# One load for K and V of the last kv head, and its softmax factors and outputs apart from those of the first seven heads

## The chip, the cores and the metric

The kernel runs on one core of one Trainium2 chip. The metric is the device time of one execution in microseconds (us). TensorE (PE in the profile; PEld is its weight load), VectorE (DVE), ScalarE (ACT), GpSimd (POOL) and SyncE (SP) run side by side, each through its own instructions in a fixed order, and wait for each other by semaphores. All loads are issued by SP and run on 16 DMA engines. All data is float32.

## The reference

One decode step of attention over a cached window, a dense block with the Mish activation beside it, and a gate that mixes the two. Two batch rows, 32 query heads on 8 kv heads, head size 128, a window of the last 4096 keys.

```python
def _A_ref(x, k_cache, v_cache, wq, wo):        # x (2, 1, 512), Hq 32, Hkv 8, Dh 128
    W = min(4096, max(256, Sk // 4))            # 4096 of 32768 keys
    rep = Hq // Hkv                             # 4
    q = ((x @ wq).reshape(B, Sq, Hq, Dh)).transpose(0, 2, 1, 3)
    k = jnp.repeat(k_cache[:, :, Sk - W:, :], rep, axis=1)
    v = jnp.repeat(v_cache[:, :, Sk - W:, :], rep, axis=1)
    scores = jnp.einsum("bhqd,bhkd->bhqk", q, k) * (Dh ** -0.5)
    p = _softmax(scores, axis=-1)
    o = jnp.einsum("bhqk,bhkd->bhqd", p, v)
    return o.transpose(0, 2, 1, 3).reshape(B, Sq, Hq * Dh) @ wo
def _B_ref(x, w1, b1, w2):                      # F 1792
    h = jnp.einsum("bsd,df->bsf", x, w1) + b1
    sp = jnp.log1p(jnp.exp(-jnp.abs(h))) + jnp.where(h > 0, h, jnp.zeros_like(h))
    return jnp.einsum("bsf,fd->bsd", h * jnp.tanh(sp), w2)
g = _sigmoid((x * gate_w).sum(-1, keepdims=True))
return g * a + (1 - g) * b
```

## The kernel before, in words

**Loads.** The pool `stream` has three buffers of 64 KB per partition. In order of issue they take: wq; K and V of kv heads 0 to 6 (`kv0` to `kv6`, each one load of 128 rows of 64 KB); `w12`, which is w1 and ten of the fourteen slabs of w2 (rows of 48 KB); `kv7`, which is K of the last head (rows of 32 KB) and then V of it (another 32 KB); and `wo` in three loads for kv heads 0 to 3, 4 to 6 and 7 (`WO`, rows of 32, 24 and 8 KB). Three small loads of the last slabs of w2 come last, into the free end of w12's buffer (L282). A load of a buffer waits until the last matmul on what the buffer held is done: `wo` waits for the values of `kv6`. SP issues everything, so the order of the loads is the order of the program.

**One kv head.** `scores` (L137) multiplies the queries with K, 16 matmuls in groups of four: four matmuls stand in four column groups of 32 of the array (`Q * j`) and run side by side. The profile shows each float32 matmul as two records, so a group of four is eight. VectorE takes the row maximum (`mx`), ScalarE the exponential and the row sum (`p`, `ls`). `turned` (L149) transposes p by four matmuls into `pp`, and ScalarE copies it to `pT`. `values` (L162) multiplies pT with V, 16 matmuls in groups of four, into half of a two-head tile of PSUM; after an odd head VectorE picks the valid part of both heads (`om`, L175) and sums it (`od`, L178).

**The softmax across pieces.** A row of a head is spread over several pieces with a maximum of their own. `tops` (L181) transposes the maxima of all eight heads (`mt`), copies them (`ms`), takes the common one (`mj`, `top`), subtracts on GpSimd and takes the exponential; `factors` (L197) transposes that back (`ft`) into `kf` and `kl`; `shares` (L208) sums by a matmul (`lp`) and inverts (`r`); `outputs` (L217) does one small matmul per head (`ol`) and scales into `oT`.

**The end.** `hidden` (L225) does the first layer of the dense block as w12 lands. Then, in an order that is written out by hand and pinned on TensorE (`pin`): scores of head 7, five slabs of w2 (`middle`), `tops`, the transposes of head 7, five slabs of w2, `factors`, the values of head 7 with `shares` in between, `outputs`, and 32 matmuls of oT with wo (`project`, L290; four query heads to a kv head, again four side by side). The sum `acc` is copied (`asum`), added up over its four column groups together with the last four slabs of w2 (`fin`), copied to `res` and stored.

Of the kernel before, what the change touches and what calls it, by code (L numbers as in the profile page):

```python
# [20 lines left out]
DH = 128
W = min(4096, max(256, SK // 4))
NH = 2
# [15 lines left out]
CAP = 20.0  # L39
CUTS = (0, 10, 12, 13, 14)  # L40
WO = (0, 4, 7, 8)


@with_exitstack
def decode_kernel(ctx: ExitStack, tc: tile.TileContext, res, stored, small, wqh, wqt, kv_in, w12, k7, v7, wo, w2, out):
    nc = tc.nc

    stream = ctx.enter_context(tc.tile_pool(name="stream", bufs=3))
# [8 lines left out]
    def load(name, *parts):  # L57
        t = stream.tile([P, 2 * CHUNK], F32, tag="s", name=name)
        x = 0
        for cols, src in parts:  # L60
            loads.append(nc.sync.dma_start(t[:, x : x + cols], src))  # L61
            x += cols
        return t
# [93 lines left out]
    def softmax(kv, t):  # L157
        return turned(kv, scores(kv, t))

    pair = [None]  # L160

    def values(kv, pT, t, c0=0, c1=NT):  # L162
        if kv % 2 == 0:
            pair[0] = ps_1.tile([P, 2, BN * DH], F32, tag="o", name=f"o{kv}")
        o = pair[0][:, kv % 2, :]
        for c in range(c0, c1):
            for j in range(NJ):
                pin(nc.tensor.matmul(o[Q * j : Q * j + Q], pT[:, c, Q * j : Q * j + Q],  # L168
                                     t[:, (c * NJ + j) * 512 : (c * NJ + j + 1) * 512],
                                     start=(c == 0), stop=(c == NT - 1)))  # L170
        if kv % 2 and c1 == NT:
            wide = [P, 2 * BN, DH]
            om = single.tile(wide, F32, tag="om", name=f"om{kv}")
            ov = om.rearrange("p (k m) d -> p k m d", m=BN)
            nc.vector.tensor_tensor(  # L175
                ov, pair[0].rearrange("p k (m d) -> p k m d", m=BN),
                pick[:, None, :, None].to_broadcast([P, 2, BN, DH]), op=ALU.mult)
            nc.vector.tensor_reduce(od[:, kv - 1 : kv + 1], ov.rearrange("p k m d -> p k d m"),  # L178
                                    axis=AX.X, op=ALU.add)

    def tops():  # L181
        mt = ps_1.tile([HKV, NJ, Q], F32, tag="q", name="mt")
        pin(nc.tensor.transpose(mt.rearrange("k j r -> k (j r)"), mx, ident))
        ms = const.tile([HKV, NJ, Q], F32, name="ms")
        nc.scalar.copy(ms, mt)
        m4 = ms.rearrange("k j (y n h) -> k j y n h", n=NH, h=REP)
        mj = const.tile([HKV, NJ, Q // NH // REP, REP], F32, name="mj")
        nc.vector.tensor_tensor(mj, m4[:, :, :, 0, :], m4[:, :, :, 1, :], op=ALU.min)
        top = const.tile([HKV, Q // NH // REP, REP], F32, name="top")
        nc.vector.tensor_reduce(top, mj.rearrange("k j y h -> k y h j"), axis=AX.X, op=ALU.min)  # L190
        for n in range(NH):
            nc.gpsimd.tensor_tensor(m4[:, :, :, n, :], m4[:, :, :, n, :],
                                    top[:, None].to_broadcast(mj.shape), op=ALU.subtract)
        nc.scalar.activation(ms, ms, AF.Exp, scale=-1.0)
        return ms

    def factors(ms):  # L197
        ft = ps_1.tile([P, HKV], F32, tag="q", name="ft")
        pin(nc.tensor.transpose(ft, ms.rearrange("k j r -> k (j r)"), ident[:HKV, :HKV]))
        wide = [P, HKV, BH]  # L200
        kb = key.rearrange("p b h -> p (b h)")[:, None, :].to_broadcast(wide)
        kf = const.tile(wide, F32, name="kf")
        kl = const.tile(wide, F32, name="kl")
        nc.vector.tensor_tensor(kf, kb, ft[:, :, None].to_broadcast(wide), op=ALU.mult)
        nc.vector.tensor_tensor(kl, kf, ls[:, :, None].to_broadcast(wide), op=ALU.mult)
        return kf, kl

    def shares(kl):  # L208
        lp = ps_1.tile([P, HKV, B, REP], F32, tag="q", name="lp")
        pin(nc.tensor.matmul(lp.rearrange("p k b h -> p (k b h)"), ones,  # L210
                             kl.rearrange("p k x -> p (k x)"), start=True, stop=True))
        r = const.tile([P, HKV, B, REP], F32, name="r")
        nc.vector.reciprocal(r, lp)
        nc.gpsimd.tensor_tensor(r, r, g[:, None, :, None].to_broadcast([P, HKV, B, REP]), op=ALU.mult)
        return r

    def outputs(ol, kf, r, k0, k1):  # L217
        for kv in range(k0, k1):
            pin(nc.tensor.matmul(ol[:, kv].rearrange("p b h -> p (b h)"), od[:, kv, :], kf[:, kv, :],  # L219
                                 start=True, stop=True))  # L220
        nc.vector.tensor_tensor(
            oT.rearrange("p (k h) (b x) -> p k b h x", h=REP, x=RS)[:, k0:k1, :, :, 0],
            ol[:, k0:k1], r[:, k0:k1], op=ALU.mult)

    def hidden(t):  # L225
        w = t[:, : DC * F].rearrange("p (c f) -> p c f", c=DC)
        hp = ps_s.tile([P, FG * P], F32, tag="sc", name="hp")
        for c in range(DC):
            for j in range(NJ):
                n = min(FG, FC - j * FG) * P  # L230
                nc.tensor.matmul(hp[Q * j : Q * j + Q, :n], x32[:, c, :],  # L231
                                 w[:, c, j * FG * P : j * FG * P + n],
                                 start=(c == 0), stop=(c == DC - 1))
        hs = work.tile([P, FG * P], F32, tag="p", name="hs")
        nl = (FC - (NJ - 1) * FG) * P
# [24 lines left out]
        nc.gpsimd.tensor_scalar_add(de, nu, 2.0)  # L260
        nc.vector.reciprocal(de, de)
        nc.gpsimd.tensor_tensor(nu, nu, de, op=ALU.mult)
        nc.gpsimd.tensor_tensor(actT[:, :, ::RS], nu, ho, op=ALU.mult)
# [1 line left out]
    queries(0, wq_t[:, :CHUNK])  # L265
    queries(1, wq_t[:, CHUNK:])

    for kv in range(HKV - 1):
        t = load(f"kv{kv}", (2 * CHUNK, kv_in[kv]))
        pT = softmax(kv, t[:, :CHUNK])  # L270
        values(kv, pT, t[:, CHUNK:])
    w12_t = load("w12", (DC * F + CUTS[1] * D, w12))
    last = load("kv7", (CHUNK, k7), (CHUNK, v7))

    def flat(src, cuts, size):
        for f0, f1 in zip(cuts, cuts[1:]):
# [4 lines left out]
    for cols, src in flat(w2, [f - CUTS[1] for f in CUTS[1:]], D):  # L281
        loads.append(nc.sync.dma_start(w12_t[:, x : x + cols], src))  # L282
        x += cols
    hidden(w12_t)

    acc = ps_1.tile([P, D], F32, tag="acc", name="acc")
    fin = ps_1.tile([P, P], F32, tag="fin", name="fin")
# [19 lines left out]
            x = DC * F + f * D  # L307
            pin(project(f % NJ, actT[:, f, :], w12_t[:, x : x + D], n_of[f % NJ]))

    p = scores(HKV - 1, last[:, :CHUNK])  # L310
    middle(0, CUTS[1] // 2)
    ms = tops()
    pT = turned(HKV - 1, p)
    middle(CUTS[1] // 2, CUTS[1])
    kf, kl = factors(ms)
    values(HKV - 1, pT, last[:, CHUNK:], 0, 1)
    r = shares(kl)
    values(HKV - 1, pT, last[:, CHUNK:], 1, NT)
    ol = ps_1.tile([P, HKV, B, REP], F32, tag="q", name="ol")
    outputs(ol, kf, r, 0, HKV - 2)  # L320
    outputs(ol, kf, r, HKV - 2, HKV)
    for x in range(HQ):
        project(x % REP, oT[:, x, :], wo_t[:, x * D : (x + 1) * D], n_of[x % REP])
    asum = work.tile([P, D], F32, tag="p", name="asum")
    nc.scalar.copy(asum[:, : D // 2], acc[:, : D // 2])
    nc.vector.tensor_copy(asum[:, D // 2 :], acc[:, D // 2 :])
# [76 lines left out]
```

## Time and profile before

| what | value |
|---|---|
| median of 3 runs | 219.33 us (219.29 to 219.65) |
| the profiled execution, its own time | 219.44 us |
| its span in the profile | 217.6 us, so 1.84 us lie around it |
| bytes moved | 91.40 MB, mean 420 GB/s over the span |
| busy: PE | 119.1 us (55%) |
| busy: PEld, DVE, ACT, POOL | 34.6, 21.9, 15.4 and 7.5 us |

Times in the rows below are microseconds from the start of the span. A row of the timeline gives start, length, engine, line, operation, what is written and read, the shapes, how many records are merged, and in brackets how long the engine had been idle and what ended that. The length of a merged row runs from its first start to its last end. A matmul's end is modelled, so of matmuls the starts are read first. The granted clock is a share of 2.4 GHz.

### The profile page before, as it was taken

The page shows a single profiled execution, that of the slowest core. Times are in us where ns is not written, and L with a number is a line of the kernel's source. Part 1 is how long each engine was busy: PE and PEld are TensorE (multiplying, and loading weights), DVE is VectorE, ACT ScalarE, POOL GpSimd, SP SyncE. Part 2 cuts the span into 40 slices and gives each one's busy share as a digit, 9 for nine tenths or more (in the row PEclk, how much of TensorE's full clock was granted, in tenths as well). Part 3 has the DMA queues.
Part 4 walks back from the last instruction along what each step waited for, and adds up shares of the span by engine and source line. Part 5 has one row for each costly group of instructions (what it writes and reads, how often), then busy time and mean ns, then how long its engine had stood idle before and what let it go on. Part 6 is the DMA issues. An engine that isn't in the chain of part 4 may idle for free.

```text
span 217.6 us, 1803 instructions
## 1 busy us (share of the span) xinstructions
PE 119.1 (55%) x804; PEld 34.6 (16%) x804; DVE 21.9 (10%) x34; ACT 15.4 (7%) x34; POOL 7.5 (3%) x29
## 2 busy tenths in 40 slices
PE   0000788287046609573670755296465572996876
PEld 0000322012011102111110111012011120233212
DVE  0000000010001140100114010000501000125001
ACT  2000011002001100200110020002002010120000
POOL 7000000000000000000000000000000002010000
PEclk9999999679758965888898599567969998899599
DMA  9797988898989899989898989898999899999993
GB/s 361 337 506 337 581 386 386 386 569 386 398 386 566 386 389 398 554 386 410 386 545 386 422 386 542 386 422 386 497 434 434 349 476 392 473 392 461 411 389 133
DMA packets 2886, 91.40 MB, mean 420 GB/s; under 512 B 448, under 2 KB 576, under 8 KB 960
## 3 DMA queue, kind: packets, MB, share of 16 engines
q1 hardware_dynamic: 2880, 91.31, 97.5%
q8 instruction: 6, 0.10, 0.2%
HBM read 91.24 MB, written 0.07 MB: 420 GB/s over the span
## 4 chain that ended last, share of the span: by engine, by line
DMA 79%; PE 16%; ACT 2%; DVE 1%; SPq 1%; issue 1%; ACTq 0%
DMA kv<-in_kv 61%; DMA wo<-in_wo 18%; PE sc L141 8%; PE o L168 5%; PE acc L292 2%; ACT p L146 1%; DVE mx L144 1%; PE pp L153 1%; ACT pT L154 1%; PE fin L301 1%; SPq L61 1%; SPq L67 0%; DVE res L343 0%; ACTq L154 0%; ACTq L146 0%
## 5 line engine op out<-in xcount | busy, mean ns | idle before, releaser
L141 PE MATMUL sc<-kv,qz 128*32 128x512 f32 x256 | 46.2, 887 | 47.5 <-DMA kv<-in_kv 42.6
L168 PE MATMUL o<-kv,pT 128*32 128x512 f32 x256 | 32.3, 646 | 5.2 <-ACT pT L154 5.1
L121 PE MATMUL qp<-wq,x 128*32 128x512 f32 x64 | 10.6, 709 | 23.0 <-POOL x L89 23.0
L141 PEld LDWEIGHTS sc<-kv,qz 128*32 128x32 f32 x256 | 10.2, 155 | 81.8 <-DMA kv<-in_kv 48.3
L144 DVE TENSOR_REDUCE mx<-sc 128x1 f32<-128x512 f32 x8 | 5.5, 691 | 101.1 <-PE sc L141 101.1
L146 ACT ACTIVATE p<-sc,mx 128x512 f32<-128x512 f32 x8 | 5.5, 687 | 125.2 <-DVE mx L144 125.2
L168 PEld LDWEIGHTS o<-kv,pT 128*32 128x32 f32 x256 | 7.8, 118 | 23.3 <-issue 16.3
L153 PE MATMUL pp<-ident,p 128*128 128x128 f32 x32 | 5.2, 285 | 11.6 <-ACT p L146 11.6
L292 PE MATMUL acc<-wo,oT 128*32 128x512 f32 x64 | 9.4, 737 | 2.5 <-DMA wo<-in_wo 2.5
L178 DVE TENSOR_REDUCE od<-om 128x256 f32<-128x1024 f32 x4 | 7.5, 1882 | 0.1
L175 DVE TENSOR_TENSOR om<-o,pick 128x1024 f32<-128x1024 f32 x4 | 4.9, 1224 | 21.6 <-PE o L168 21.6
L121 PEld LDWEIGHTS qp<-wq,x 128*32 128x32 f32 x64 | 2.3, 126 | 28.1 <-POOL x L89 23.0
L153 PEld LDWEIGHTS pp<-ident,p 128*128 128x128 f32 x32 | 3.4, 141 | 18.3 <-ACT p L146 18.3
L255 POOL TENSOR_SCALAR e<-h 128x28 f32<-128x28 f32 x1 | 0.3, 286 | 151.3 <-DVE h L250 151.3
L154 ACT COPY pT<-pp 128x512 f32<-128x512 f32 x8 | 4.7, 585 | 5.8 <-PE pp L153 5.8
L231 PE MATMUL hp<-w,x 128*32 128x512 f32 (+1 forms) x32 | 3.6, 543 | 2.5 <-DMA w<-in_w 2.5
L292 PE MATMUL acc<-w,actT 128*32 128x512 f32 x20 | 3.8, 597 | 0.0
L219 PE MATMUL ol<-kf,od 128*128 128x8 f32 x16 | 2.5, 285 | 2.2 <-DVE od L178 2.2
L292 PEld LDWEIGHTS acc<-wo,oT 128*32 128x32 f32 x64 | 2.2, 130 | 8.9 <-issue 4.8
L219 PEld LDWEIGHTS ol<-kf,od 128*128 128x128 f32 x16 | 2.3, 224 | 3.1 <-DVE od L178 2.3
L110 DVE RECIPROCAL g<-g 128x2 f32<-128x2 f32 x1 | 0.2, 165 | 23.0 <-POOL g L109 23.0
L127 PE MATMUL qt<-ident,qs 128*128 128x128 f32 x8 | 1.3, 286 | 1.4 <-ACT qs L124 1.4
(65 smaller groups left out, 30.4 us busy)
## 6 DMA issues: line engine op xcount, KB each, us to landing
wq<-in_wqt SPq DMA_DIRECT2D x1, 7168.0 KB, 21.4
w<-in_w SPq DMA_DIRECT2D x1, 6144.0 KB, 40.5
kv<-in_k SPq DMA_DIRECT2D x1, 4096.0 KB, 28.8
kv<-in_v SPq DMA_DIRECT2D x1, 4096.0 KB, 38.1
wo<-in_wo SPq DMA_DIRECT2D x1, 4096.0 KB, 31.4
wo<-in_wo SPq DMA_DIRECT2D x1, 3072.0 KB, 38.4
wq<-in_wqh SPq DMA_DIRECT2D x1, 1024.0 KB, 4.9
wo<-in_wo SPq DMA_DIRECT2D x1, 1024.0 KB, 40.3
```

Source lines behind the costliest of these rows:

```text
L121: nc.tensor.matmul(qp[Q * k : Q * k + Q, :], x32[:, c, :], w[:, c, k, :], start=(c == 0), stop=(c == DC - 1))
L141: nc.tensor.matmul(sc[Q * j : Q * j + Q, :], qz[:, kv, m * Q : m * Q + Q], t[:, (m * NJ + j) * 512 : (m * NJ + j + 1) * 512], start=(m == ...
L144: nc.vector.tensor_reduce(mx[:, kv : kv + 1], sc, axis=AX.X, op=ALU.max, negate=True)
L146: nc.scalar.activation(p, sc, AF.Exp, bias=mx[:, kv : kv + 1], accum_out=ls[:, kv : kv + 1])
L153: pin(nc.tensor.transpose(pp[:, c, :], p[:, c * P : (c + 1) * P], ident))
L154: nc.scalar.copy(pT, pp)
L168: pin(nc.tensor.matmul(o[Q * j : Q * j + Q], pT[:, c, Q * j : Q * j + Q], t[:, (c * NJ + j) * 512 : (c * NJ + j + 1) * 512], start=(c == 0 ...
L175: nc.vector.tensor_tensor(ov, pair[0].rearrange("p k (m d) -> p k m d", m=BN), pick[:, None, :, None].to_broadcast([P, 2, BN, DH]), op=ALU ...
L178: nc.vector.tensor_reduce(od[:, kv - 1 : kv + 1], ov.rearrange("p k m d -> p k d m"), axis=AX.X, op=ALU.add)
L219: pin(nc.tensor.matmul(ol[:, kv].rearrange("p b h -> p (b h)"), od[:, kv, :], kf[:, kv, :], start=True, stop=True))
L231: nc.tensor.matmul(hp[Q * j : Q * j + Q, :n], x32[:, c, :], w[:, c, j * FG * P : j * FG * P + n], start=(c == 0), stop=(c == DC - 1))
L292: return nc.tensor.matmul(acc[Q * j : Q * j + Q, :], lhsT, rhs, start=(n_col[j] == 1), stop=(n_col[j] == n))
```

## The change

K and V of head 7 become one load of 64 KB rows, as for the other heads; the inputs `k7` and `v7` go. `tops`, `factors`, `shares` and `outputs` take a range of heads. They run once for heads 0 to 6, after `hidden` and ahead of the scores of head 7, and once for head 7 alone. Head 6 is picked and summed by itself (`PICKED`), as is head 7. In the pinned order of TensorE the ten slabs of w2 are cut in 4, 3 and 3 instead of 5 and 5, and the 16 matmuls with wo of kv heads 0 to 3 stand ahead of the `ol` of head 7.

```diff
+PICKED = (1, 3, 5, 6, 7)
...
-        if kv % 2 and c1 == NT:
-            wide = [P, 2 * BN, DH]
...
+        if c1 == NT:
+            held[1] += 1
+            if kv in PICKED:
+                picked(kv, held[1])
+                held[1] = 0
+
+    def picked(kv, n):
+        om = single.tile([P, n * BN, DH], F32, tag="om", name=f"om{kv}")
+        ov = om.rearrange("p (k m) d -> p k m d", m=BN)
+        nc.vector.tensor_tensor(
+            ov, held[0][:, :n].rearrange("p k (m d) -> p k m d", m=BN),
+            pick[:, None, :, None].to_broadcast([P, n, BN, DH]), op=ALU.mult)
+        nc.vector.tensor_reduce(od[:, kv + 1 - n : kv + 1], ov.rearrange("p k m d -> p k d m"),
+                                axis=AX.X, op=ALU.add)
...
-    last = load("kv7", (CHUNK, k7), (CHUNK, v7))
+    last_t = load(f"kv{last}", (2 * CHUNK, kv_in[last]))
...
     hidden(w12_t)
 
+    kf, kl = factors(tops(0, last), 0, last)
+    outputs(kf, shares(kl, 0, last), 0, last)
+
...
-    p = scores(HKV - 1, last[:, :CHUNK])
-    middle(0, CUTS[1] // 2)
-    ms = tops()
-    pT = turned(HKV - 1, p)
-    middle(CUTS[1] // 2, CUTS[1])
-    kf, kl = factors(ms)
-    values(HKV - 1, pT, last[:, CHUNK:], 0, 1)
-    r = shares(kl)
-    values(HKV - 1, pT, last[:, CHUNK:], 1, NT)
-    ol = ps_1.tile([P, HKV, B, REP], F32, tag="q", name="ol")
-    outputs(ol, kf, r, 0, HKV - 2)
-    outputs(ol, kf, r, HKV - 2, HKV)
-    for x in range(HQ):
-        project(x % REP, oT[:, x, :], wo_t[:, x * D : (x + 1) * D], n_of[x % REP])
+    def heads(k0, k1):
+        for x in range(k0 * REP, k1 * REP):
+            pin(project(x % REP, oT[:, x, :], wo_t[:, x * D : (x + 1) * D], n_of[x % REP]))
+
+    p = scores(last, last_t[:, :CHUNK])
+    middle(0, 4)
+    ms = tops(last, HKV)
+    middle(4, 7)
+    pT = turned(last, p)
+    middle(7, CUTS[1])
+    kf, kl = factors(ms, last, HKV)
+    values(last, pT, last_t[:, CHUNK:], 0, 1)
+    r = shares(kl, last, HKV)
+    values(last, pT, last_t[:, CHUNK:], 1, NT)
+    heads(0, WO[1])
+    outputs(kf, r, last, HKV)
+    heads(WO[1], HKV)
```

On TensorE, from the transposes of the dense block (`ht`) to the matmuls with wo, before. The names are those above, with numbers; `mt`, `ft`, `lp` and `ol` belong to the softmax across pieces, `acc<-w` is `middle`, `acc<-wo` the product with wo:

```order
L246 MATMUL ht<-ident,hs 128x96 x2
L141 MATMUL sc_553<-kv_500,qz 32x512 x16
L292 MATMUL acc<-w_498,actT 32x512 x5
L183 MATMUL mt<-ident,mx 8x128
L153 MATMUL pp_589<-ident,p_571 128x128 x4
L292 MATMUL acc<-w_498,actT 32x512 x5
L199 MATMUL ft<-ident,ms 128x8
L168 MATMUL o_481<-kv_500,pT_590 32x512 x4
L210 MATMUL lp<-kl,ones 128x64
L168 MATMUL o_481<-kv_500,pT_590 32x512 x12
L219 MATMUL ol<-kf,od 128x8 x8
L292 MATMUL acc<-wo,oT 32x512 x32
```

The same place now, in two pieces. The first runs from the transposes of the dense block to the scores of head 7:

```order
L256 MATMUL ht<-ident,hs 128x96 x2
L190 MATMUL mt_553<-ident,mx 7x128
L207 MATMUL ft_564<-ident,ms_555 128x7
L219 MATMUL lp_570<-kl_567,ones 128x56
L229 MATMUL ol_575<-kf_566,od 128x8 x7
L142 MATMUL sc_586<-kv_503,qz 32x512 x16
```

The second runs from there to the matmuls with wo:

```order
L306 MATMUL acc<-w_501,actT 32x512 x4
L190 MATMUL mt_610<-ident,mx 1x128
L306 MATMUL acc<-w_501,actT 32x512 x3
L154 MATMUL pp_624<-ident,p_604 128x128 x4
L306 MATMUL acc<-w_501,actT 32x512 x3
L207 MATMUL ft_634<-ident,ms_612 128x1
L169 MATMUL o_640<-kv_503,pT_625 32x512 x4
L219 MATMUL lp_645<-kl_637,ones 128x8
L169 MATMUL o_640<-kv_503,pT_625 32x512 x12
L306 MATMUL acc<-wo,oT 32x512 x16
L229 MATMUL ol_681<-kf_636,od 128x8
L306 MATMUL acc<-wo,oT 32x512 x16
```

The softmax across pieces stands there twice, for seven heads ahead of the scores of head 7 and for one head after them, and the last `ol` has moved into the middle of the matmuls with wo.

On ScalarE, from the exponential of the dense block to the copy of the sum, before:

```order
L256 ACTIVATE e<-e 128x28
L146 ACTIVATE p_571,ls<-sc_553,mx 128x512
L185 COPY ms<-mt 8x128
L154 COPY pT_590<-pp_589 128x512
L194 ACTIVATE ms<-ms 8x128
L325 COPY asum<-acc 128x256
```

The same place now:

```order
L266 ACTIVATE e<-e 128x28
L201 ACTIVATE ms_555<-ms_555 7x128
L147 ACTIVATE p_604,ls<-sc_586,mx 128x512
L192 COPY ms_612<-mt_610 1x128
L201 ACTIVATE ms_612<-ms_612 1x128
L155 COPY pT_625<-pp_624 128x512
L342 COPY asum<-acc 128x256
```

The copy `pT` of head 7 stood ahead of the exponential of `ms` and stands behind it now.

## Rows read from the trace of the kernel before

**Rows 1.** DMA queue (packets, MB, share of 16 engines); one transfer's KB, issue to landing.

```profile
q1 hardware_dynamic: 2880, 91.31, 97.5%
...
out<-res SPq DMA_DIRECT2D x1, 64.0 KB, 1.5
```

**Rows 2.** Chain of waits, the last stretch: start, length, what.

```profile
171.79 38.35 DMA wo<-in_wo
...
210.18 3.64 PE acc L292 x32
...
213.85 0.88 PE fin L301 x20
```

**Rows 3.** Timeline of PE: the scores of the eight kv heads.

```profile
42.05 5.93 PE L141 MATMUL sc<-kv,qz 128*32 128x512 f32 x32 [3.98 <-DMA kv<-in_kv]
...
62.63 5.88 PE L141 MATMUL sc<-kv,qz 128*32 128x512 f32 x32 [7.97 <-DMA kv<-in_kv]
...
82.08 6.40 PE L141 MATMUL sc<-kv,qz 128*32 128x512 f32 x32 [6.84 <-DMA kv<-in_kv]
...
101.39 5.28 PE L141 MATMUL sc<-kv,qz 128*32 128x512 f32 x32 [4.79 <-DMA kv<-in_kv]
...
120.79 5.82 PE L141 MATMUL sc<-kv,qz 128*32 128x512 f32 x32 [7.45 <-DMA kv<-in_kv]
...
140.09 6.40 PE L141 MATMUL sc<-kv,qz 128*32 128x512 f32 x32 [6.83 <-DMA kv<-in_kv]
...
159.40 5.29 PE L141 MATMUL sc<-kv,qz 128*32 128x512 f32 x32 [4.77 <-DMA kv<-in_kv]
...
183.55 5.16 PE L141 MATMUL sc<-kv,qz 128*32 128x512 f32 x32 [4.88 <-DMA kv<-in_k]
```

**Rows 4.** Timeline of PE: starts that a landing released (w12, V of head 7, wo).

```profile
173.88 3.63 PE L231 MATMUL hp<-w,x 128*32 128x512 f32 x32 [2.53 <-DMA w<-in_w]
...
193.23 1.06 PE L168 MATMUL o<-kv,pT 128*32 128x512 f32 x8 [0.18 <-DMA kv<-in_v]
...
202.90 5.72 PE L292 MATMUL acc<-wo,oT 128*32 128x512 f32 x32 [0.91 <-DMA wo<-in_wo]
```

**Rows 5.** Stretches: length; busy PE, PEld, DVE, ACT, POOL; granted clock; DMA share; GB/s.

```profile
183.60:186.40 2.80, 2.80 (x16) 0.75 (x20) 0.00 (x0) 0.00 (x0) 0.00 (x0) 0.50 0.95 410
...
193.30:198.80 5.50, 5.50 (x46) 2.48 (x46) 2.02 (x4) 0.00 (x0) 0.29 (x1) 1.00 1.06 459
203.00:206.90 3.90, 3.90 (x20) 0.89 (x24) 0.00 (x0) 0.00 (x0) 0.00 (x0) 0.50 0.98 422
...
210.20:213.80 3.60, 3.60 (x32) 0.92 (x32) 0.00 (x0) 0.00 (x0) 0.00 (x0) 1.00 0.90 364
```

**Rows 6.** Timeline of all engines, from the scores of head 7 to its outputs.

```profile
190.16 0.19 ACT L146 ACTIVATION_READ_ACCUMULATOR p<-sc,mx 128x1 f32 x1
...
190.66 0.26 ACT L185 COPY ms<-mt 8x128 f32<-8x128 f32 x1 [0.31 <-PE mt L183]
...
191.16 0.59 ACT L154 COPY pT<-pp 128x512 f32<-128x512 f32 x1 [0.24 <-PE pp L153]
...
192.21 0.31 ACT L194 ACTIVATE ms<-ms 8x128 f32<-8x128 f32 x1 [0.47 <-POOL ms L192]
...
194.23 0.43 PE L210 MATMUL lp<-kl,ones 128*128 128x64 f32 x2
...
194.59 2.78 PE L168 MATMUL o<-kv,pT 128*32 128x512 f32 x24
...
197.31 1.42 PEld L219 LDWEIGHTS ol<-kf,od 128*128 128x128 f32 x12 [0.84 <-issue]
...
197.44 1.23 DVE L175 TENSOR_TENSOR om<-o,pick 128x1024 f32<-128x1024 f32 x1 [2.19 <-PE o L168]
199.04 1.88 DVE L178 TENSOR_REDUCE od<-om 128x256 f32<-128x1024 f32 x1
...
200.97 1.02 PE L219 MATMUL ol<-kf,od 128*128 128x8 f32 x4 [2.16 <-DVE od L178]
```

More of the change, by code (lines that the diff above doesn't have):

```diff
@@ L41, with decode_kernel @@
 WO = (0, 4, 7, 8)
+PICKED = (1, 3, 5, 6, 7)
 @with_exitstack
-def decode_kernel(ctx: ExitStack, tc: tile.TileContext, res, stored, small, wqh, wqt, kv_in, w12, k7, v7, wo, w2, out):
+def decode_kernel(ctx: ExitStack, tc: tile.TileContext, res, stored, small, wqh, wqt, kv_in, w12, wo, w2, out):
     nc = tc.nc
@@ L158, in softmax @@
         return turned(kv, scores(kv, t))
-    pair = [None]
+    held = [None, 0]
     def values(kv, pT, t, c0=0, c1=NT):
-        if kv % 2 == 0:
-            pair[0] = ps_1.tile([P, 2, BN * DH], F32, tag="o", name=f"o{kv}")
-        o = pair[0][:, kv % 2, :]
+        if c0 == 0 and held[1] == 0:
+            held[0] = ps_1.tile([P, 2, BN * DH], F32, tag="o", name=f"o{kv}")
+        o = held[0][:, held[1], :]
         for c in range(c0, c1):
@@ L181, in tops @@
[L181 to L184, printed above, removed]
+        if c1 == NT:
[11 more added lines that the diff above has]
+                                axis=AX.X, op=ALU.add)
@@ L185, in tops @@
+    def tops(k0, k1):
+        n = k1 - k0
+        mt = ps_1.tile([n, NJ, Q], F32, tag="q", name=f"mt{k0}")
+        pin(nc.tensor.transpose(mt.rearrange("k j r -> k (j r)"), mx[:, k0:k1], ident))
+        ms = const.tile([n, NJ, Q], F32, name=f"ms{k0}")
         nc.scalar.copy(ms, mt)
         m4 = ms.rearrange("k j (y n h) -> k j y n h", n=NH, h=REP)
-        mj = const.tile([HKV, NJ, Q // NH // REP, REP], F32, name="mj")
+        mj = const.tile([n, NJ, Q // NH // REP, REP], F32, name=f"mj{k0}")
@@ L188, in tops @@
         nc.vector.tensor_tensor(mj, m4[:, :, :, 0, :], m4[:, :, :, 1, :], op=ALU.min)
-        top = const.tile([HKV, Q // NH // REP, REP], F32, name="top")
+        top = const.tile([n, Q // NH // REP, REP], F32, name=f"top{k0}")
         nc.vector.tensor_reduce(top, mj.rearrange("k j y h -> k y h j"), axis=AX.X, op=ALU.min)
-        for n in range(NH):
-            nc.gpsimd.tensor_tensor(m4[:, :, :, n, :], m4[:, :, :, n, :],
+        for i in range(NH):
+            nc.gpsimd.tensor_tensor(m4[:, :, :, i, :], m4[:, :, :, i, :],
@@ L195, in tops, with factors, shares, outputs @@
         return ms
[L197 to L200, printed above, removed]
+    def factors(ms, k0, k1):
+        n = k1 - k0
+        ft = ps_1.tile([P, n], F32, tag="q", name=f"ft{k0}")
+        pin(nc.tensor.transpose(ft, ms.rearrange("k j r -> k (j r)"), ident[:n, :n]))
+        wide = [P, n, BH]
         kb = key.rearrange("p b h -> p (b h)")[:, None, :].to_broadcast(wide)
-        kf = const.tile(wide, F32, name="kf")
-        kl = const.tile(wide, F32, name="kl")
+        kf = const.tile(wide, F32, name=f"kf{k0}")
+        kl = const.tile(wide, F32, name=f"kl{k0}")
         nc.vector.tensor_tensor(kf, kb, ft[:, :, None].to_broadcast(wide), op=ALU.mult)
-        nc.vector.tensor_tensor(kl, kf, ls[:, :, None].to_broadcast(wide), op=ALU.mult)
+        nc.vector.tensor_tensor(kl, kf, ls[:, k0:k1, None].to_broadcast(wide), op=ALU.mult)
         return kf, kl
-    def shares(kl):
-        lp = ps_1.tile([P, HKV, B, REP], F32, tag="q", name="lp")
+    def shares(kl, k0, k1):
+        wide = [P, k1 - k0, B, REP]
+        lp = ps_1.tile(wide, F32, tag="q", name=f"lp{k0}")
         pin(nc.tensor.matmul(lp.rearrange("p k b h -> p (k b h)"), ones,
                              kl.rearrange("p k x -> p (k x)"), start=True, stop=True))
-        r = const.tile([P, HKV, B, REP], F32, name="r")
+        r = const.tile(wide, F32, name=f"r{k0}")
         nc.vector.reciprocal(r, lp)
-        nc.gpsimd.tensor_tensor(r, r, g[:, None, :, None].to_broadcast([P, HKV, B, REP]), op=ALU.mult)
+        nc.gpsimd.tensor_tensor(r, r, g[:, None, :, None].to_broadcast(wide), op=ALU.mult)
         return r
-    def outputs(ol, kf, r, k0, k1):
+    def outputs(kf, r, k0, k1):
+        ol = ps_1.tile([P, k1 - k0, B, REP], F32, tag="q", name=f"ol{k0}")
         for kv in range(k0, k1):
-            pin(nc.tensor.matmul(ol[:, kv].rearrange("p b h -> p (b h)"), od[:, kv, :], kf[:, kv, :],
+            pin(nc.tensor.matmul(ol[:, kv - k0].rearrange("p b h -> p (b h)"), od[:, kv, :], kf[:, kv - k0, :],
                                  start=True, stop=True))
@@ L222, in outputs @@
             oT.rearrange("p (k h) (b x) -> p k b h x", h=REP, x=RS)[:, k0:k1, :, :, 0],
-            ol[:, k0:k1], r[:, k0:k1], op=ALU.mult)
+            ol, r, op=ALU.mult)
     def hidden(t):
@@ L266, in decode_kernel @@
     queries(1, wq_t[:, CHUNK:])
-    for kv in range(HKV - 1):
+    last = HKV - 1
+    for kv in range(last):
         t = load(f"kv{kv}", (2 * CHUNK, kv_in[kv]))
@@ L382 @@
         "wqt": c(wq[:, HEAD:]),
-        "kv": c(np.concatenate([kt[:-1], vt[:-1]], axis=2)),
+        "kv": c(np.concatenate([kt, vt], axis=2)),
         "w12": c(np.concatenate([w1, w2_0], axis=1)),
-        "k7": c(kt[-1]),
-        "v7": c(vt[-1]),
         "wo": c(wo),
```

7 lines of the change are left out of this document (removed).

## The prediction

> **What bounds the kernel now.** I read the DMA queues first, then the last stretch of the chain of waits, then the timeline of TensorE, and last the timeline of all engines around head 7. The queues show a program that is one stream of loads: their packets fill 97.5% of the span [rows 1]. The chain says the same, and it says where the stream stops being the limit: it is a DMA until 210.14, when the second load of wo lands, and from 210.18 it is TensorE with 32 records (16 matmuls), then `fin` [rows 2]. So the end stands at a fixed distance behind that landing, as long as TensorE is ready by 210.18. Before, it is ready: the matmuls of the first load of wo start when that load lands, at 202.90, though the engine was free 0.91 before it, and are done with 1.56 us to spare ahead of 210.18, even at half clock [rows 4 and 5]. (202.90 + 5.72 = 208.62.) That slack of 1.56 us is what the change can spend before it costs anything, and there is no more to win than an earlier landing.
>
> **The loads.** K of head 7 lands at 183.55, V at 193.23; w12 landed at 173.88 [rows 3 and 4]. K took 9.67 us and V 9.68, together 19.35 for two loads of 32 KB rows. The loads of 64 KB rows took 19.45, 19.31, 19.40, 19.30 and 19.31 from kv1's start to kv6's, 19.35 in the mean [rows 3]. The merged load therefore lands when V landed, at 193.23, with -0.05 to +0.10 as the bounds from those five. One DMA, 128 packets and one issue on SP fewer cost and bring nothing, because the queue is full and SP has long issued everything behind it: the wait for wo's transfer begins at 171.79 [rows 2], over 20 us ahead of V's landing. wo still waits for the values of head 6, which are not touched.
>
> A rule speaks the other way. The Trainium skill (DMA: Bandwidth & Descriptors, Anatomy of one DMA) gives each DMA a fixed cost of about 2.0 us beside its bytes, fitted on another issuing path. By it, one load fewer would end the stream 2 us earlier and the sum below would be about 218.3 (an estimate from that figure); the trace does not agree, with 19.35 us for two loads and 19.35 for one.
>
> **The first seven heads.** Their part of the softmax moves into the idle time between the dense block and the landing of head 7, ahead of the scores in TensorE's order. Before, the stretch from the copy `ms` to the last of the first twelve `ol` records ran from 190.66 to 198.73, 8.1 us, with other matmuls in between [rows 6]. Put behind the dense block, whose matmuls end at 177.51 [rows 4], with an estimated 2 us for its copies and transposes, it is done by about 187.6 at the latest, 5.6 us ahead of 193.23. I cost it at nothing. Were that cover gone, the scores of head 7 would start late by what sticks out, 8.1 us at most. On VectorE, picking head 6 alone costs half an `om` and half an `od`, 1.6 us [rows 6], and nobody waits there.
>
> **Head 7: what it gives up.** Before, the scores of head 7 ran while V was still in flight: they started at 183.55 and everything up to `pT` was done by 191.75, ahead of V [rows 3 and 6]. Now they start at 193.23, and the whole softmax stands behind the landing. That is the cost. I count from the end of the scores, E; before it was 183.55 + 5.16 = 188.71.
> - p and its row sum are done at 190.35, so at E + 1.64 [rows 6]. The slabs of w2 (4, 3, 3) and the transposes run beside what follows and end at about E + 3.4, so they don't decide.
> - On ScalarE, `ms` of head 7 follows p at once, and its exponential ended 1.86 us after the copy's start (190.66 to 192.52): E + 3.53. For one partition instead of eight I take the same time, since the elements per partition are the same.
> - The copy `pT` now waits behind it on ScalarE: 0.59 us, with handing over E + 4.2 [rows 6]. Queued ahead of it is a wait on TensorE, VectorE and GpSimd; the values of head 7 wait for it. (With the old order on ScalarE, `ft` in front of the values would still wait for the same exponential, so the order alone costs some 0.3.)
> - The values: from the first group of four to the second 193.23 to 194.59, 1.36 us with `lp` between; three more groups in the 24 records behind [rows 4 and 6]. A group is 3.64 - 2.78 = 0.86 us at full clock [rows 2 and 6]. So 1.36 + 3 x 0.86 = 3.94: E + 8.14.
> - The matmuls of kv heads 0 to 3 with wo, landed at 202.90: four groups, 3.44: E + 11.58. `om` and `od` of head 7 run beside them, 1.6 us from E + 8.3, done at about E + 10.
> - `ol` of head 7: `lp`, of the same build, cost 1.36 - 0.86 = 0.50 between two groups: E + 12.08.
> - Then the 16 matmuls of kv heads 4 to 7 start, which started at 210.18 before; all that follows is unchanged.
>
> **The scores themselves.** E is not fixed. In all eight heads they begin at half the clock after an idle time of 4.0 to 8.0 us and reach the full one on the way: 1.2 GHz in the stretch from 183.60 to 186.40, 2.4 GHz by 193.30 [rows 3 and 5]. They lasted 5.16 to 6.40 us, 5.77 in the mean of eight [rows 3]. After the merged load the idle time is about as long, so they begin slow again, and the old timing, in which V hid them, is gone. With 5.77: 193.23 + 5.77 + 12.08 = 211.08, which is 0.90 us past 210.18. With the shortest it is 0.29, with the longest 1.53. For the small operations on one head I allow 0.3 us either way, so 0 to 1.8 in all; I take the mean, because nothing ties the landing of head 7 to the moment at which the clock rises.
>
> The Trainium skill (TensorE: Matmul & The Clock Gate, Part 1) says that the same kernel meets a different number of slow matmuls from run to run. The eight scores of this one trace already differ by 1.24 us, which agrees; by it the time of the changed kernel would spread more over its runs than the 0.36 us of before.
>
> The sum: 219.44 (the profiled execution's own time, of which 217.6 is span) + 0.90 = 220.3. That execution stands 0.11 above the median of 219.33, which is within the range of the runs shown.
>
> **The rivals.**
> - Hidden after all: the chain is some 0.5 us shorter than I count, or the clock rises early, and the landing at 210.14 still decides. For it speaks that three of eight scores took 5.3 us or less, and that my chain reaches 210.18 within 0.3 us with those. Against it: every term above comes from a row, and only the one-head operations could be shorter. Time 219.4.
> - Faster: each load has a part that its bytes don't explain. The store of 64 KB takes 1.5 us from issue to landing [rows 1], while its bytes at the loads' rate (8.39 MB in 19.35 us) take 0.15. If 1.35 us of this stood in the stream at each boundary, the merged load and all of wo would land 1.35 us earlier, and with the chain's 0.90 the end would be 0.45 earlier: 219.0. It decides where the saving is over 0.9 us. Against it are the intervals of one and of two loads, equal within 0.1 us. The fixed cost in the skill's DMA page, named above, is the rule for this case.
> - The clock falls again within the chain: it has waits of 0.1 to 0.8 us between E and E + 4.2, and before the clock was at half when wo's matmuls began at 202.90 [rows 5]. Those came behind idle times of 2.16 and 0.91 [rows 4 and 6], longer than any in the chain; in the values it was 1.00 from 193.30 to 198.80. Should the values and heads 0 to 3 start at half clock, the time until it rises, 3.1 us to 5.6 by the scores, counts double: 1.6 to 2.8 more, 222.5.
>
> **How the numbers follow.** My forecast has 0.64, hidden 0.22, faster 0.08, the clock 0.06. About 0.2% (0.44 us) is what a measurement of this kernel tells from no change. Of the forecast's 0.64 I give 0.07 to scores so short that the delay is under 0.44. So slower has 0.57 + 0.06 = 0.63, the same 0.22 + 0.07 = 0.29, faster 0.08. The range runs from 219.1, which takes in the hidden case and half of the faster one, to 221.4, the longest scores with 0.3 and a little more (219.44 + 1.83 = 221.3). Outside are most of the clock's case and half of the faster one, and some of the forecast's tail.
>
> **What the changed profile would show.** The scores of head 7 start at about 193.2, at half clock, with `ol` of seven heads done more than 5 us before. The copy `pT` follows the exponential of `ms` about 4.2 us after the scores' end. The matmuls of wo start at once behind the values, with no wait for a DMA; those of the second load start after 210.2, behind `ol`, with no wait for a DMA either. The chain of waits then runs back from `fin` through TensorE to the landing of kv7, and no longer to wo. I am wrong if TensorE waits again for the second load of wo at 210.1 (hidden), if the merged load lands by more than 0.3 us off 193.2, or if the clock is at half in the values.

## The result and the profile after

The changed kernel takes 220.38 us in the median of 9 runs (219.68 to 220.91), the kernel before 219.51 (219.29 to 219.65): ratio 1.0036, 95% interval 1.0025 to 1.0047. It is slower, by 0.87 us; the forecast was 220.3. The profiled execution of the changed kernel took 220.83 us, with a span of 218.7.

First the chain of waits after, its last stretch (start, length, what). It answers to [rows 2].

```profile
152.45 40.78 DMA kv<-in_kv
...
193.28 6.39 PE sc L142 x32
...
203.51 1.07 PE o L169 x8
...
207.61 3.43 PE acc L306 x32
211.04 0.32 PE ol L229 x2
211.36 3.62 PE acc L306 x32
...
215.88 0.88 PE fin L315 x20
```

The wait for wo at 210.14 is gone from the chain. What releases the end now is the landing of head 7, and behind it 22 us of TensorE nearly without a gap. The last 16 matmuls with wo take 3.6 us as before; they start 1.11 us later.

The timeline after, all engines, around head 7 (start, length, engine, line, operation, and in brackets how long the engine had been idle). It answers to [rows 3, 4 and 6].

```profile
186.45 0.25 DVE L231 TENSOR_TENSOR oT<-ol,r 128x56 f32<-128x56 f32 x1 [3.32 <-PE ol L229]
...
193.28 6.39 PE L142 MATMUL sc<-kv,qz 128*32 128x512 f32 x32 [6.93 <-DMA kv<-in_kv]
...
201.06 0.19 ACT L147 ACTIVATION_READ_ACCUMULATOR p<-sc,mx 128x1 f32 x1
201.15 0.24 ACT L192 COPY ms<-mt 1x128 f32<-1x128 f32 x1
...
202.27 1.06 PE L306 MATMUL acc<-w,actT 128*32 128x512 f32 x6
...
202.69 0.31 ACT L201 ACTIVATE ms<-ms 1x128 f32<-1x128 f32 x1 [1.30 <-POOL ms L199]
202.90 0.56 ACT L155 COPY pT<-pp 128x512 f32<-128x512 f32 x1
...
203.26 0.22 PE L207 MATMUL ft<-ident,ms 1*128 1x1 f32 x1
...
203.51 1.07 PE L169 MATMUL o<-kv,pT 128*32 128x512 f32 x8
...
207.43 3.62 PE L306 MATMUL acc<-wo,oT 128*32 128x512 f32 x32
...
210.97 0.39 PE L229 MATMUL ol<-kf,od 128*128 128x8 f32 x2
...
211.29 3.64 PE L306 MATMUL acc<-wo,oT 128*32 128x512 f32 x32
```

The first seven heads are done at 186.7, 6.5 us before the landing at 193.23. The scores start at 193.28 and end at 199.67. Neither row of the product with wo has a wait in brackets: the loads of wo had landed when TensorE got there.

Two stretches after (length; busy PE, PEld, DVE, ACT, POOL; granted clock; DMA share; GB/s). They answer to [rows 5].

```profile
193.30:198.80 5.50, 5.50 (x28) 1.36 (x32) 0.00 (x0) 0.00 (x0) 0.00 (x0) 0.50 1.09 471
199.50:214.90 15.40, 15.37 (x138) 4.74 (x134) 3.63 (x9) 1.69 (x5) 0.79 (x3) 1.00 0.92 386
```

Nearly all of the scores ran at 1.2 GHz, and everything behind them at 2.4 GHz. TensorE was busy for 15.37 of 15.40 us from the scores' end to the end of the product.

### The profile page after: what moved, and what is told of

It reads as the page before. It is cut to its first block, busy times and chain, and to the rows that moved or that the text cites. A ratio compares the mean times of both kernels' runs of the same rounds, so it can differ in the third digit from the quotient of the medians.

```text
span 218.7 us, 1827 instructions
## 1 busy us (share of the span) xinstructions
PE 119.1 (54%) x808; PEld 36.0 (16%) x808; DVE 23.4 (11%) x41; ACT 15.7 (7%) x36; POOL 8.2 (4%) x32
## 3 DMA queue, kind: packets, MB, share of 16 engines
q1 hardware_dynamic: 2736, 91.31, 96.9%
## 4 chain that ended last, share of the span: by engine, by line
DMA 69%; PE 26%; ACT 2%; DVE 1%; issue 0%; SPq 0%; POOL 0%; ACTq 0%
DMA kv<-in_kv 60%; DMA sm<-in_small 10%; PE sc L142 8%; PE qp L122 5%; PE o L169 5%; PE acc L306 5%; PE pp L154 1%; PE zp L106 1%; ACT p L147 1%; DVE mx L145 1%; ACT pT L155 1%; PE fin L315 0%; SPq L62 0%; PE qt L128 0%; ACT qs L125 0%
## 5 line engine op out<-in xcount | busy, mean ns | idle before, releaser
L122 PE MATMUL qp<-wq,x 128*32 128x512 f32 x64 | 11.7, 779 | 22.9 <-POOL x L90 22.9
L181 DVE TENSOR_TENSOR om<-o,pick 128x1024 f32<-128x1024 f32 (+1 forms) x5 | 5.1, 1012 | 29.3 <-PE o L169 29.3
L184 DVE TENSOR_REDUCE od<-om 128x256 f32<-128x1024 f32 (+1 forms) x5 | 7.8, 1560 | 0.2
L306 PE MATMUL acc<-wo,oT 128*32 128x512 f32 x64 | 7.3, 594 | 0.0
L229 PE MATMUL ol<-kf,od 128*128 128x8 f32 x16 | 3.5, 350 | 0.6 <-DVE r L222 0.6
L229 PEld LDWEIGHTS ol<-kf,od 128*128 128x128 f32 x16 | 3.4, 312 | 1.6 <-issue 0.8
L306 PE MATMUL acc<-w,actT 128*32 128x512 f32 x20 | 3.1, 600 | 0.0
```

The lines of the kernel that those rows point to most:

```text
L122: nc.tensor.matmul(qp[Q * k : Q * k + Q, :], x32[:, c, :], w[:, c, k, :], start=(c == 0), stop=(c == DC - 1))
L181: nc.vector.tensor_tensor(ov, held[0][:, :n].rearrange("p k (m d) -> p k m d", m=BN), pick[:, None, :, None].to_broadcast([P, n, BN, DH]), ...
L184: nc.vector.tensor_reduce(od[:, kv + 1 - n : kv + 1], ov.rearrange("p k m d -> p k d m"), axis=AX.X, op=ALU.add)
L229: pin(nc.tensor.matmul(ol[:, kv - k0].rearrange("p b h -> p (b h)"), od[:, kv, :], kf[:, kv - k0, :], start=True, stop=True))
L306: return nc.tensor.matmul(acc[Q * j : Q * j + Q, :], lhsT, rhs, start=(n_col[j] == 1), stop=(n_col[j] == n))
```

## The experiments

Each run of a kernel reports its time and its span, and the difference is told below as "around the span". Twelve kernels were run.

**The kernel before against itself.** No edit.

> The kernel before, unchanged, timed against itself. It asks one thing: how far time and span stand apart in it. The changed kernel's nine runs have 2.1 to 2.2 us around their spans, the one profiled run of before 1.84. Theory one (all of the delay lies in the span, in TensorE's chain behind the merged load): this kernel shows about 2.1 us around its span as well in other runs. Theory two (0.3 us of the delay lies around the span, for instance because the changed program has two inputs fewer and more instructions): this kernel keeps 1.84 us in all runs. Time 219.5 by both, all runs within 0.4 us.

It took 219.51 us, 219.29 to 219.67 in 11 runs. Around the span lay 1.82 to 1.96 us in 40 runs of the kernel before, 1.89 in the mean. In the nine runs of the changed kernel it was 2.08 to 2.18. So theory two holds for 0.24 us (the means are 2.13 and 1.89): part of the delay isn't in the span at all. Why it is there is asked further down.

**Which part makes it: two loads again, or the merged load alone.** The first kernel is the changed one with two loads; its inputs `k7` and `v7` are back as well.

```diff
...
-    last_t = load(f"kv{last}", (2 * CHUNK, kv_in[last]))
+    last_t = load(f"kv{last}", (CHUNK, k7), (CHUNK, v7))
...
```

> The changed kernel with K and V of the last head again in two loads of 32 KB rows; everything else as changed (seven heads and one head apart). Theory one (the merged load alone costs, by putting the scores of head 7 behind V's landing): the scores run while V is in flight, the values start at 193.2 with V, the matmuls of the first load of wo wait for its landing at 202.9, and the second load's wait for 210.1 as before: span 217.6, time 219.5, the spread of before. Rival (the split of the softmax and its added instructions cost): 220.0 to 220.4 as the changed kernel.

The profiled run did at its end what theory one says, but not in the middle. Its timeline of TensorE, the scores, the first values, and the two starts that a landing of wo released:

```profile
186.38 5.64 PE L142 MATMUL sc<-kv,qz 128*32 128x512 f32 x32
...
195.87 1.06 PE L169 MATMUL o<-kv,pT 128*32 128x512 f32 x8
...
202.96 5.34 PE L306 MATMUL acc<-wo,oT 128*32 128x512 f32 x32 [2.99 <-DMA wo<-in_wo]
...
210.21 3.64 PE L306 MATMUL acc<-wo,oT 128*32 128x512 f32 x32 [1.59 <-DMA wo<-in_wo]
```

The values were expected at 193.2, with V, and start at 195.87: the `ol` of the first seven heads, ahead of the scores in TensorE's order, end only at 186.4, so the scores start 2.8 us behind the start of before [rows 3]. Here the first seven heads aren't free, then; the wait of 2.99 us for wo behind them hides it.

Six of twelve runs took 219.65 to 219.86, with spans of 217.5 to 217.8, as the kernel before. The other six took 221.41 to 222.86, with spans of 219.3 to 220.7. Neither theory had foreseen this, and the median, 220.64 (ratio 1.0064, 1.0034 to 1.0094), says little. Around the span lay 2.06 to 2.20 us, in both groups, so the 0.24 us come with the split of the softmax; the next kernel shows that they don't come with the merged load.

The other half alone, the merged load with the old order:

```diff
...
-    last = load("kv7", (CHUNK, k7), (CHUNK, v7))
+    last = load("kv7", (2 * CHUNK, kv_in[HKV - 1]))
...
```

> The kernel before with K and V of the last head in one load of 64 KB rows, and the old order of everything else (one softmax across all eight heads behind the last scores). Theory one: the whole of the old tail now stands behind the landing at 193.2: scores to 199.0, values to about 207.5, picking and summing two heads to about 211, then some 27 of the 32 matmuls with wo at 0.21 us each, so that the product with wo ends at about 218.1 instead of 213.8: 4.3 us slower, 223.8 (223 to 225). Rival (a load of 64 KB rows saves something at a boundary between loads): the second load of wo lands earlier than 210.1 by 0.5 us or more.

It took 223.28 us (222.58 to 223.91; ratio 1.0176, 1.0159 to 1.0193), with 1.86 to 1.91 around the span. Its chain of waits:

```profile
192.99 5.83 PE sc L141 x32
...
208.77 0.25 DVE oT L221
...
211.51 5.40 PE acc L292 x49
...
217.23 0.45 PE acc L292 x3
```

The product with wo ends at 217.68 (forecast 218.1), 3.86 us later than before. The load landed at 192.94, 0.3 us ahead of V's landing before [rows 4]. The second load of wo took 38.1 us from issue to landing, 38.4 before, and was issued 0.2 us later: no transfer came earlier by 0.5 us, and the rival falls. Against this kernel the rest of the change, the split and the new order, gives back 2.9 us.

**The clock of the scores.** 16 added matmuls ahead of the scores of head 7, on resident data; their result is overwritten.

```diff
+WARM = 16
...
+    for i in range(WARM):
+        j = i % NJ
+        pin(nc.tensor.matmul(acc[Q * j : Q * j + Q, :], x32[:, 0, :], w12_t[:, j * D : (j + 1) * D],
+                             start=True, stop=True))
...
```

> The changed kernel with 16 more matmuls on TensorE, on data that lies there, between the output matmuls of the first seven heads and the scores of head 7; their result is overwritten. Theory one (the delay and its spread come from scores that start at half clock): TensorE runs them from about 186.4 to 190 or 193, the scores start at full clock and last about 3.6 us instead of 5.2 to 6.4, the product with the second load of wo waits for 210.1 again: span 217.6, and the runs lie within 0.5 us of each other: 219.5. Rival (the chain is too long at any clock): the matmuls of the second load of wo still start behind 210.3 with no wait, 219.9 or more. Third (the clock falls again before the landing): scores of 5 us or more and the time of the changed kernel, 220.4.

The profiled run, TensorE's timeline:

```profile
193.03 3.64 PE L143 MATMUL sc<-kv,qz 128*32 128x512 f32 x32 [0.49 <-DMA kv<-in_kv]
...
210.07 3.64 PE L311 MATMUL acc<-wo,oT 128*32 128x512 f32 x32 [1.72 <-DMA wo<-in_wo]
```

The scores take 3.64 us instead of 6.39, at a clock of 1.00 from 193.05 on, and the wait for wo is back. Ten of twelve runs took 219.43 to 219.86, with spans of 217.3 to 217.7: as theory one says, plus the 0.24 around the span. Two runs took 221.32 and 221.88. The median is 219.77 (ratio 1.0023, 1.0004 to 1.0042). By the medians, adding work to TensorE made the kernel faster by 0.6 us. The intervals of the two ratios overlap, though, because of the two long runs; with four matmuls more, below, they don't.

**A shorter chain, with the slabs of w2 ahead.**

```diff
+    middle(0, CUTS[1])
     p = scores(last, last_t[:, :CHUNK])
-    middle(0, 4)
+    pT = turned(last, p)
     ms = tops(last, HKV)
-    middle(4, 7)
-    pT = turned(last, p)
-    middle(7, CUTS[1])
+    values(last, pT, last_t[:, CHUNK:], 0, 2)
     kf, kl = factors(ms, last, HKV)
-    values(last, pT, last_t[:, CHUNK:], 0, 1)
+    values(last, pT, last_t[:, CHUNK:], 2, 3)
     r = shares(kl, last, HKV)
-    values(last, pT, last_t[:, CHUNK:], 1, NT)
+    values(last, pT, last_t[:, CHUNK:], 3, NT)
```

> The changed kernel with the ten slabs of w2 ahead of the scores of head 7 instead of behind them, and the copy pT ahead of the softmax across pieces on ScalarE (ft and lp stand among the values). The chain behind the merged load gets shorter: the values start at about 3.1 us behind the scores' end instead of 3.84. Theory one (the delay is the length of TensorE's chain behind the landing): heads 4 to 7 are ready by 208 to 210.4 and wait for the load of wo in most runs, 219.7 at best. Theory two, beside it (a wait in front of the last 16 matmuls costs the clock): the runs fall into two groups, some at 219.6 to 219.9 and some at 221 to 222.5, as with two loads, although the chain is shorter. Rival (the slabs behind the scores were hidden): the values start as before at 3.8 us behind the scores' end, and the time stays 220.4.

TensorE's timeline of the profiled run:

```profile
193.30 5.21 PE L142 MATMUL sc<-kv,qz 128*32 128x512 f32 x32 [2.71 <-DMA kv<-in_kv]
...
201.47 1.92 PE L169 MATMUL o<-kv,pT 128*32 128x512 f32 x16 [0.57 <-ACT pT L155]
...
210.21 3.66 PE L306 MATMUL acc<-wo,oT 128*32 128x512 f32 x32 [0.60 <-DMA wo<-in_wo]
```

The values start 2.96 us behind the scores' end (198.51), 0.88 sooner than in the changed kernel. Seven of eleven runs took 219.70 to 220.43, four 221.44 to 222.11; the median is 220.19 (ratio 1.0054, 1.0029 to 1.0078). Both theories hold: a shorter chain, and a second group of runs with it. Three things were changed at once (the slabs, the place of `pT`, and `ft` and `lp` among the values), so how the 0.88 divides between them isn't told apart.

**The second group of runs.** Three kernels ask what it is. The first adds four matmuls to the one with 16 ahead of the scores, in the wait for the second load of wo (`fill` issues matmuls as above into a free tile of PSUM):

```diff
     outputs(kf, r, last, HKV)
+    fill(4, "f1")
     heads(WO[1], HKV)
```

> The kernel with 16 added matmuls ahead of the scores of head 7, and four more behind the last output matmul, ahead of the last 16 matmuls with wo; their result is not used. Without these four, two of twelve runs took 221.3 and 221.9 against 219.4 to 219.9 in the others. Theory (in those runs the clock fell in the 1.7 us of waiting for the second load of wo, and the last 16 matmuls ran at half clock): the slow group goes, all runs lie at 219.4 to 219.9. Rival (those runs are slow from something earlier, as scores that start at half clock): two groups remain.

All eleven runs took 219.70 to 220.17, median 219.87 (ratio 1.0015, 1.0007 to 1.0024). The second group is gone, and the interval lies just below that of the changed kernel (1.0025 to 1.0047): with 20 matmuls more the kernel is faster. In the profiled run the added matmuls stand at 208.48 and the wait behind them is 0.82:

```profile
208.48 1.07 PE L338 MATMUL f<-w,x 128*32 128x512 f32 x8
...
210.37 3.64 PE L311 MATMUL acc<-wo,oT 128*32 128x512 f32 x32 [0.82 <-DMA wo<-in_wo]
```

The second does the same for the kernel with two loads, in both of its waits:

```diff
+    fill(12, "f0")
     heads(0, WO[1])
     outputs(kf, r, last, HKV)
+    fill(12, "f1")
     heads(WO[1], HKV)
```

> The kernel with K and V in two loads and the split softmax, with twelve added matmuls ahead of the first 16 matmuls with wo and twelve ahead of the last 16; their result is not used. Without them six of twelve runs took 221.4 to 222.9, the others 219.7 to 219.9. Theory (the product with the first load of wo runs at full clock in those runs, is done by 207, and in the 3.4 us of waiting for the second load the clock falls, so that the last 16 matmuls take up to twice their 3.4 us): the slow group goes, all runs at 219.5 to 220.0. Rival (the slow group has to do with the loads or with the split): two groups remain, median 220.6.

All eight runs took 219.79 to 220.25, median 219.98 (ratio 1.0022, 1.0013 to 1.0032), where six of twelve had taken over 221.4.

The third keeps the first filling of that kernel and leaves out the second:

```diff
-    fill(12, "f1")
```

> The kernel with K and V in two loads, the split softmax, and added matmuls only ahead of the first 16 matmuls with wo, so that these run at full clock in every run and are done by about 207; in front of the last 16 nothing is added. Theory (waiting some 3.3 us for the second load of wo drops the clock, and the last 16 matmuls then run at half clock until it rises): the slow group becomes the rule, 221.4 to 223.2 in most runs, and the profile shows a granted clock of 0.50 from 210.2 on and more than 3.64 us for the last 32 records. Rival (the slow group came from something earlier, which the first filling removed): 219.5 to 220.0 in all runs and a clock of 1.00 there.

Eight of ten runs took 221.15 to 222.93, two 219.53 and 219.55; the median is 221.41 (ratio 1.0073, 1.0044 to 1.0101, without the longest run). This time the profile caught one of the eight. TensorE's timeline:

```profile
203.25 3.62 PE L306 MATMUL acc<-wo,oT 128*32 128x512 f32 x32
206.80 0.39 PE L229 MATMUL ol<-kf,od 128*128 128x8 f32 x2
210.18 5.34 PE L306 MATMUL acc<-wo,oT 128*32 128x512 f32 x32 [2.99 <-DMA wo<-in_wo]
```

And its stretches, with the clock as the last number but two:

```profile
203.00:206.40 3.40, 3.40 (x38) 0.95 (x32) 0.00 (x0) 0.00 (x0) 0.00 (x0) 1.00 0.98 417
207.00:210.10 3.10, 0.19 (x2) 0.10 (x1) 0.17 (x1) 0.00 (x0) 0.00 (x0) 1.00 0.89 381
210.30:212.50 2.20, 2.20 (x20) 0.61 (x20) 0.00 (x0) 0.00 (x0) 0.00 (x0) 0.76 0.97 398
212.50:213.50 1.00, 1.00 (x12) 0.33 (x8) 0.00 (x0) 0.00 (x0) 0.00 (x0) 0.50 0.80 313
213.50:214.50 1.00, 1.00 (x8) 0.22 (x4) 0.00 (x0) 0.00 (x0) 0.00 (x0) 0.50 0.39 152
```

The first product with wo runs at 2.4 GHz and is done early. TensorE waits 2.99 us, the clock falls, and the last 16 matmuls, on which the end hangs, take 5.34 us instead of 3.64. The place where it fell is not where I had put it: it was still 1.00 through the wait and until 211.40, and in shorter stretches 0.54 from 211.40 to 211.70 and 0.50 behind that, with matmuls running. Except for that, the theory holds, and the rival falls. The profiled run with two loads and no filling shows the same one product earlier: behind its 2.99 us of waiting the clock was 1.00 from 202.96 to 203.80 and 0.50 from 204.20, and those 16 matmuls took 5.34 us too, but there the next landing left time for it.

**Where the 0.24 us around the span come from.** It isn't the merged load and not the number of inputs: with nine inputs and the split it was 2.06 to 2.20, with seven and the merged load alone 1.86 to 1.91. The split adds seven instructions on VectorE, three on GpSimd, two on ScalarE and three small matmuls. The first three numbers were each added alone to the kernel before, as tiny copies in the dense block:

```diff
+        junk = const.tile([P, 8, B], F32, name="junk")
+        for i in range(7):
+            nc.vector.tensor_copy(junk[:, i], h[:, i])
```

> The kernel before with seven tiny copies more on VectorE in the dense block (their result is not used): as many instructions as the split adds there. All kernels with the split have 2.07 to 2.20 us around their span, all without it 1.82 to 1.96. Theory (the longer program of VectorE costs the 0.25 us): about 2.13 us around the span, time 219.7. Otherwise 1.89 us and 219.5.

> The kernel before with three tiny copies more on GpSimd in the dense block (their result is not used): as many instructions as the split adds there. If the longer program of GpSimd costs the 0.25 us around the span: about 2.13 us there, time 219.8. Otherwise 1.89 us and 219.5 to 219.6.

> The kernel before with two tiny copies more on ScalarE in the dense block (their result is not used): as many instructions as the split adds there. If the longer program of ScalarE costs the 0.25 us around the span: about 2.13 us there, time 219.7. Otherwise 1.89 us and 219.5.

They took 219.50, 219.58 and 219.52 us, with 1.83 to 1.91, 1.83 to 1.93 and 1.83 to 1.94 around the span. None is the cause by itself; all together weren't tried. More matmuls aren't it either: the last kernel below has 20 more than the kernel before and 1.83 to 1.92 around its span. Which property of the split costs the 0.24 us stays open.

**A try at a kernel faster than both.** wo is cut at another place, and TensorE's waits ahead of its product are filled.

```diff
-WO = (0, 4, 7, 8)
+WO = (0, 5, 7, 8)
...
+    fill(8, "f0")
     outputs(ol, kf, r, HKV - 2, HKV)
+    fill(12, "f1")
     for x in range(HQ):
-        project(x % REP, oT[:, x, :], wo_t[:, x * D : (x + 1) * D], n_of[x % REP])
+        pin(project(x % REP, oT[:, x, :], wo_t[:, x * D : (x + 1) * D], n_of[x % REP]))
```

> The kernel before (two loads, one softmax) with wo cut behind kv heads 5 and 7 instead of 4 and 7, and eight and twelve added matmuls in TensorE's two idle times ahead of the product with wo, so that it starts at full clock. Theory (the end stands 16 matmuls, 3.4 us, behind the landing of the second load of wo at 210.1): now eight matmuls stand behind that landing and four behind the third load's at 212.6; the product ends at about 213.5 instead of 213.8, so 0.3 us faster: 219.2. Rival (the last loads of w2 decide): no change, 219.5. Third (the first load, now larger, lands at 205.3, and its 20 matmuls run at half clock): slower, 220.5 or more.

It took 219.50 us (219.29 to 219.67), ratio 0.9996, interval 0.9987 to 1.0004: no change. Its timeline of TensorE:

```profile
205.54 4.50 PE L292 MATMUL acc<-wo,oT 128*32 128x512 f32 x40 [0.92 <-DMA wo<-in_wo]
210.38 1.92 PE L292 MATMUL acc<-wo,oT 128*32 128x512 f32 x16 [0.34 <-DMA wo<-in_wo]
212.83 1.06 PE L292 MATMUL acc<-wo,oT 128*32 128x512 f32 x8 [0.53 <-DMA wo<-in_wo]
```

and the end of its chain of waits:

```profile
173.03 40.98 DMA w<-in_w
...
214.05 1.74 PE fin L301 x40
```

The 20 matmuls ran at full clock (1.00 from 205.6 to 210.0) and TensorE waited for each load of wo. The product ended at 213.89 and not at the 213.5 expected, because its last four matmuls had to wait for the third load, until 212.83; and then w2 landed, at 214.01. The stream of loads is the limit to its very end here, as the rival said. The kernel before had it so already: its product ends at 213.82, and the weight load behind it waits for w2.

```profile
213.85 0.38 PEld L301 LDWEIGHTS fin<-w,actT 128*32 128x32 f32 x16 [0.93 <-DMA w<-in_w]
```

So an earlier end of the product alone had next to nothing to win. No kernel that was run beats the one before.

## Why the prediction was right

The direction, the time and the place were right: the loads didn't change, the chain of head 7 behind one landing took the place of the wait for wo, and its price hung on the clock of the scores. Point by point, with the profiled run:

- The loads. For the merged one 193.23 was forecast, with -0.05 to +0.10, and 193.23 found (the scores start at 193.28). The second load of wo was issued 2.4 us later than before and took 36.0 us to land instead of 38.4, so it landed as before. The queue has 144 packets fewer (2736 against 2880), not 128. The Trainium skill's fixed cost for each DMA (DMA: Bandwidth & Descriptors, Anatomy of one DMA) doesn't show in these landings; the kernel with the merged load alone has it at 192.94, 0.3 us earlier and not 2.
- The first seven heads cost nothing in the span: done at 186.7, forecast 187.6 at the latest.
- The scores: forecast 5.77 with 5.16 to 6.40 as ends, found 6.39, at half clock until nearly their end (0.50 from 193.30 to 198.80). That the clock carries the cost is shown by the 16 added matmuls, which took 2.75 us off the scores and brought the wait for wo back into the chain.
- The step that was mis-sized: "the copy `pT` now waits behind it ... with handing over E + 4.2". The values started at E + 3.84. The copy of `ms` began at 201.15, before the reading of the row sum ended at 201.25, and not after it; the copy `pT` began 0.10 before the exponential ended, and was ready at 203.46. It was also not ScalarE alone that decided: TensorE had its slabs of w2 until 203.33 and `ft` until 203.48. I had written that the slabs end at E + 3.4 and don't decide; with `ft` they end together with `pT`.
- From the values to the second product with wo I counted 7.88 us (3.94, 3.44, 0.50) and 7.78 were found. The whole chain behind the scores took 11.62 instead of 12.08.
- The sum in the span: 193.28 + 6.39 + 11.62 = 211.29, which is 1.11 past 210.18, where I had 0.90. Over the nine runs the spans are 217.5 to 218.8, 218.2 in the median, which is 0.6 more than 217.6.
- What I left out: 0.24 us around the span. It is a term of the sum that the forecast has at nothing; 0.6 + 0.24 is 0.84 of the 0.87 found. So the median agrees with the forecast partly by luck: two errors, a chain too long by 0.46 and this, cancel.
- The spread: forecast as larger than the 0.36 us of before, and it is 1.23 (219.68 to 220.91). The Trainium skill's sentence that the same kernel meets a different number of slow matmuls from run to run (TensorE: Matmul & The Clock Gate, Part 1) agrees with this. In the kernel with 20 added matmuls, with the scores at full clock, the spread was 0.47 (219.70 to 220.17). In three of the nine runs the span was 217.5 to 217.7, as before: by that the rival "hidden after all" took place in them, though no profile shows one.
- The rival "the clock falls again" didn't occur in the changed kernel's profiled chain, which leaves TensorE no wait: a clock of 1.00 from 199.5 to 214.9. It did occur, at another place, in kernels made from it: around the last matmuls, where TensorE has to wait for wo again. One profile shows it; for the kernel with two loads and the one with 16 matmuls, the filling that took the second group away says the same; for the one with the slabs ahead it is only argued.

## What to carry to other kernels

Where a stream of loads sets the time, splitting the last load can cost nothing on the queue (here 19.35 us for two loads and for one) and lets work run while the rest is in flight; merging it puts that work behind the landing. Count the chain behind the last landings engine by engine against the next landing, with the matmuls at the clock that their rows show (here half, after waits of 4 to 8 us). And work that is finished early in front of a critical stretch may make it slower: look at the granted clock there, time several runs, and fill the wait if it matters.

## What was not expected of the hardware

- The clock came down behind a wait, not in it, in the kernel with the first filling alone: 1.00 from 207.0 to 210.1 with TensorE idle for nearly all of it, 0.76 and 0.50 in the stretches from 210.3 and 212.5 with TensorE busy throughout. Two shorter waits went the other way. With the slabs ahead, in the 2.71 us before the scores, it was 1.00 until 193.0 and 0.66 from there to 193.3; in the kernel before, in the 2.16 us before 200.97, it was 0.85 from 199.0 to 200.9 and 0.50 behind. The length of a wait alone didn't tell where the clock fell.
- The runs of one kernel, with two loads, fell into two groups, 219.65 to 219.86 and 221.41 to 222.86 us; 24 added matmuls took the second away and brought the median from 220.64 to 219.98.
- Kernels with the split have 2.06 to 2.21 us around their span (72 of 73 runs, the other 2.47), those without it 1.82 to 1.96 (142 runs), and 12 to 24 added matmuls change neither.
